# A newly searched order of steps for a fused linear-attention and gated-convolution kernel

## The chip, the cores and the metric

The kernel runs on one core of a Trainium2 chip. The metric is the device time of one execution in microseconds. Five engines work side by side, each through its own instructions in order: TensorE (PE, matmuls and the loading of their weights), VectorE (DVE), ScalarE (ACT), GpSimd (POOL) and SyncE (SP), which here only issues transfers. Transfers are carried out by 16 DMA engines. The profile is one execution recorded by the hardware profiler.

## The reference

For each of 8 batches there is an attention over 8 heads, 576 positions and head dimension 64, in which the scores are replaced by features; its result goes through a gated long convolution.

```python
def phi(x):
    proj = np.einsum('bhsd,df->bhsf', x, w_phi)                  # 64 -> 128
    proj = proj - np.max(np.abs(proj), axis=-1, keepdims=True)
    return np.concatenate([np.exp(proj), np.exp(-proj)], axis=-1)
q_p, k_p = phi(q), phi(k)
kv  = np.einsum('bhsf,bhsd->bhfd', k_p, v)
z   = np.sum(k_p, axis=2)
num = np.einsum('bhsf,bhfd->bhsd', q_p, kv)
den = np.einsum('bhsf,bhf->bhs', q_p, z)[..., None] + 1e-06
x   = (num / den) -> (8, 576, 512)

proj = x @ w_proj                                                # 512 -> 3 * 512
x1, x2, x3 = the three thirds of proj
x2_conv = irfft(rfft(x2, axis=1) * rfft(filter_fft, axis=0), n=576, axis=1)
out = (x1 * x2_conv * x3) @ w_out                                # (8, 576, 512)
```

Inputs and output are float32; the kernel computes its matmuls in bfloat16.

## The kernel before

The kernel is a list of words, `PLAN`, written out in full at the top of the file. Each word is the name of a small method with its arguments, and after an `@` the PSUM bank that it writes or reads. `run()` goes through the list once and calls them, so the list is the order in which every engine gets its instructions. Within one engine nothing overtakes; between engines an instruction waits only for what it reads or overwrites.

```python
for word in PLAN.split():
    name, _, bank = word.partition("@")
    self.bank = int(bank) if bank else None
    f, *args = name.split(",")
    getattr(self, f)(*[int(a) if a.isdigit() else a for a in args])
```

The first number of a word is the batch. Words that name an engine (`ACT`, `DVE`, `POOL`, `SP`) run there; the others have a fixed engine. The steps of one batch b, with the lines that the profile gives for them:

- `load` (L555), `loadh` (L561), `w_load` (L545, L548): q, k, v and the weights come from HBM, converted to bfloat16, by transfers that GpSimd issues. q, k, v have two buffers each.
- `trh` (L567): half of q or k is transposed by a DMA that SyncE issues; for batch 0 TensorE does it (`pt`, L577) and an engine copies the result out (`pte`, L296 on ScalarE, L298 on VectorE, which are the copies of all steps).
- `Pk`, `Qn` (L596, L603), `Pkt`, `Qnt` (L611): feature projections in the natural layout; `maxk`, `maxq`, `maxkt`, `maxqt` (VectorE, L672) take the maxima of the absolute values, `ex`, `exkt`, `exqt` (ScalarE, L658, L661, L666) the exponentials. `mhi`, `mlo`, `trm`, `trme` bring the maxima of q into rows. `Pq`, `Pqt` (L630, L636, L643, L647) project q again, transposed, with the maxima subtracted.
- `em` (L708) and `vs` (L714): v is scaled by the exponential of the maximum.
- `KV` (L729), `KVe` (copy), `NE`, `NEt` (L743, L752): the two contractions of the attention; `rc`, `xn`, `rct`, `xnt` (VectorE, L757 to L774) divide. The result x of the batch lies in four tiles `xn` and a smaller `xnt`.
- `trx` (L781), `trxt` (L786): x is transposed into `xT`, `xTt` by DMAs that SyncE issues. `ptx` (L791), `ptxt` (L800) do the same on TensorE, with `ptxe`, `ptxte` as copies out of PSUM.
- `f1`, `f2` (L811, L817): sums and differences of x; `F` (L823, L827), or `Ft` and `Fs` (L836, L843) for two tiles together: the transform along the positions; `Fe`, `Xl` copy it.
- `X2` (L862) projects in the frequency domain, `Y1` (L867, L872) multiplies by the filter's transform, `m3` (L876) adds.
- `X1`, `X3` (L884), `X1t`, `X3t` (L893) project x for the gates, with `X1e`, `X1te` (copies) and `tm`, `tmt` (L925, L929), which multiply. Each X1 and each X3 reads all four transposed tiles of the batch.
- `I` (L937), or `It` and `Is` (L944, L951): inverse transform, then `Ie` (L955, ScalarE), `Ip`, `Im` (L958, VectorE) and `ym` (L1003). `J` (L993) does the inverse with ten matmuls instead of six and needs only `yj` (L997) after it.
- `O` (L1014), `Oe` (copy), `st` (L1023): output projection, copy, and two half stores, issued by SyncE, the last five by ScalarE.

`wz` (L315) multiplies zeros by zeros, twice per word; its number is only a label. Before the first batch the kernel also builds the cosine and sine matrices of the transforms and transforms the filter (`ang`, `frac`, `sin`, `Hd`, `He`, `fa`, `hg`).

The batches overlap: while one batch's convolution runs, the attention of the next one or two is under way.

Of the kernel before, what the change touches and what calls it, by code (L numbers as in the profile page):

```python
# [49 lines left out]
fa,POOL,1 ptx,0,2@7 rc,0,0@0 ex,k,p,1,0@4 NEt,0@2 xn,0,0@0 rct,0@2 ptxe,ACT,0,2@7 ptx,0,0@6  # L50
xnt,0,1@2 ptx,0,3@4 xnt,0,0@2 Pk,1,3@0 ptxe,ACT,0,3@4 ptxe,DVE,0,0@6 fa,POOL,0 Pkt,1@2 Qn,1,2@6
X1,0,3@4 maxq,1,2@6 sin,4 X1,0,0@5 maxk,1,3@0 load,k,2 Hd,1@6 w_load,proj,1 Hd,0@7 X1e,DVE,0,3@4
exkt,m,1@2 He,DVE,1,1@6 f1,POOL,0,0,0 X3,0,0@4 X1e,ACT,0,0@5 He,DVE,1,0@6 exkt,p,1@2 Hd,2@5
ex,k,p,1,3@0 f1,POOL,0,0,1 f1,DVE,0,1,0 Hd,3@6 He,ACT,2,0@5 f1,POOL,0,1,1 ex,k,m,1,3@0 maxkt,1@2
tm,0,0@4 Pk,1,2@2 hg,ACT X1,0,2@0 f2,POOL,0,0,0 maxk,1,2@2 Qn,1,1@4 f2,POOL,0,0,1 He,DVE,3,0@6
Hd,4@1 ex,k,m,1,2@2 f2,DVE,0,1,1 em,m,1,0 em,p,1,0 ex,k,p,1,2@2 f2,DVE,0,1,0 vs,POOL,p,1,0
X1e,DVE,0,2@0 trh,k,2,0 He,ACT,3,1@6 maxq,1,1@4 X3,0,3@0 He,ACT,0,0@7 trh,k,2,1 em,p,1,1
He,ACT,4,0@1 F,0,3@4 vs,POOL,m,1,0 tm,0,3@0 F,0,1@6 Fe,ACT,0,3@4 ptxt,0@1 F,0,0@2 trh,q,2,0
Fe,ACT,0,1@6 F,0,2@4 ptxte,ACT,0@1 Fe,DVE,0,0@2 em,m,1,1 mhi,1 load,v,2 Fe,ACT,0,2@4 Pk,2,0@6
Pk,2,1@2 trh,q,2,1 KV,1,0@0 maxk,2,0@6 Xl,ACT,0 gen_ends,POOL maxk,2,1@2 X2,0,1@4 ex,k,p,2,0@6  # L60
mlo,POOL,1 load,k,3 X2,0,0@5 ex,k,m,2,0@6 KVe,DVE,1,0@0 vs,POOL,m,1,1 late Y1,0,1@4 Pkt,2@0 trm,1@6
X2,0,3@7 trme,ACT,1@6 exkt,m,2@0 Y1,0,0@5 X2,0,4@4 ex,k,p,2,1@2 w_load,out X2,0,2@6 maxkt,2@0
ex,k,m,2,1@2 vs,POOL,p,1,1 Y1,0,4@4 X1t,0@5 exkt,p,2@0 Y1,0,2@6 Pq,1,0@2 em,m,2,0 Pq,1,1@0
ex,q,m,1,0@2 X1te,DVE,0@5 X3,0,2@4 m3,POOL,0,0 Y1,0,3@7 ex,q,p,1,0@2 X1,0,1@5 tm,0,2@4 ex,q,p,1,1@0
Pq,1,2@2 m3,DVE,0,1 load,k,4 Qn,2,1@6 ex,q,m,1,1@0 X3,0,1@4 maxq,2,1@6 vs,POOL,m,2,0 X1e,ACT,0,1@5
NE,1,0@0 ex,q,m,1,2@2 tm,0,1@4 X3t,0@5 I,0,0@6 rc,1,0@0 tmt,0@5 xn,1,0@0 Ie,0,0@6 I,0,1@4 Im,0,0@6
trx,1,0 Ie,0,1@4 I,0,2@0 Ip,0,0@6 ex,q,p,1,2@2 Im,0,1@4 ym,POOL,0,0 NE,1,1@6 Ip,0,1@4 Ie,0,2@0
Pq,1,3@4 em,p,2,0 rc,1,1@6 xn,1,1@6 KV,1,1@2 load,q,3 ex,q,m,1,3@4 Im,0,2@0 trx,1,1 vs,POOL,p,2,0
Ip,0,2@0 Pk,2,2@6 ex,q,p,1,3@4 J,0,3@0 maxk,2,2@6 KVe,ACT,1,1@2 NE,1,3@2 ex,k,p,2,2@6 ym,POOL,0,2
yj,0,3@0 NE,1,2@4 rc,1,3@2 ex,k,m,2,2@6 KV,2,0@0 rc,1,2@4 xn,1,3@2 ym,POOL,0,1 xn,1,2@4 trx,1,3  # L70
Qn,2,0@6 Pqt,1@2 KVe,ACT,2,0@0 f1,POOL,1,1,1 maxq,2,0@6 O,0,3@4 exqt,m,1@2 trx,1,2 exqt,p,1@2
Pk,2,3@0 f1,POOL,1,0,0 Qnt,2@6 Qn,2,3@2 ex,k,p,2,3@0 maxqt,2@6 O,0,0@5 f1,POOL,1,0,1 maxq,2,3@2
Oe,ACT,0,3@4 trh,q,3,0 O,0,2@6 f1,DVE,1,1,0 O,0,1@4 Oe,ACT,0,2@6 f2,DVE,1,0,0 f2,POOL,1,1,1
trh,q,3,1 maxk,2,3@0 Oe,ACT,0,0@5 NEt,1@2 Oe,ACT,0,1@4 Qn,2,2@5 f2,POOL,1,1,0 rct,1@2 X1,1,3@7
trh,k,3,1 ex,k,m,2,3@0 xnt,1,0@2 xnt,1,1@2 X1,1,2@4 maxq,2,2@5 f2,POOL,1,0,1 X1e,ACT,1,3@7
st,SP,0,3,0 F,1,2@0 X1e,DVE,1,2@4 trh,k,3,0 mhi,2 F,1,3@6 Fe,ACT,1,2@0 mlo,DVE,2 F,1,0@2
Fe,DVE,1,3@6 em,p,2,1 trm,2@0 F,1,1@4 vs,POOL,p,2,1 trxt,1 trme,ACT,2@0 Fe,DVE,1,0@2 Pq,2,1@6
Fe,ACT,1,1@4 Qn,3,2@0 Qn,3,0@2 ex,q,p,2,1@6 st,SP,0,1,0 maxq,3,2@0 X2,1,2@4 st,SP,0,3,1 load,v,3
ex,q,m,2,1@6 X2,1,0@5 maxq,3,0@2 load,q,4 em,m,2,1 Pq,2,0@6 vs,POOL,m,2,1 Y1,1,0@5 Pq,2,2@0
ex,q,p,2,0@6 X2,1,3@2 Y1,1,2@4 ex,q,m,2,0@6 X2,1,1@5 ex,q,p,2,2@0 Y1,1,3@2 NE,2,0@6 X1,1,1@4  # L80
ex,q,m,2,2@0 Y1,1,1@5 m3,POOL,1,1 X3,1,2@2 Xl,ACT,1 X1e,ACT,1,1@4 NE,2,1@0 tm,1,2@2 Pkt,3@4
X3,1,3@3 rc,2,0@6 exkt,p,3@4 rc,2,1@0 xn,2,0@6 exkt,m,3@4 X1,1,0@2 xn,2,1@0 trx,2,0 tm,1,3@3
f1,POOL,2,0,0 Pqt,2@0 maxkt,3@4 KV,2,1@6 trx,2,1 exqt,p,2@0 m3,POOL,1,0 exqt,m,2@0 Pq,2,3@4
X1e,ACT,1,0@2 trh,k,4,1 Pk,3,1@0 ex,q,m,2,3@4 X2,1,4@2 maxk,3,1@0 f1,POOL,2,0,1 KVe,ACT,2,1@6
X3,1,0@3 st,SP,0,2,0 Y1,1,4@2 ex,q,p,2,3@4 NE,2,2@6 f2,POOL,2,0,1 tm,1,0@3 ex,k,m,3,1@0 X3,1,1@2
rc,2,2@6 xn,2,2@6 I,1,1@4 f2,POOL,2,0,0 tm,1,1@2 trx,2,2 Ie,1,1@4 NE,2,3@6 ex,k,p,3,1@0 Ip,1,1@4
X1t,1@2 rc,2,3@6 Im,1,1@4 X3t,1@3 X1te,ACT,1@2 xn,2,3@6 NEt,2@4 tmt,1@3 I,1,0@0 trx,2,3 rct,2@4
ym,POOL,1,1 xnt,2,1@4 Ie,1,0@0 I,1,3@6 xnt,2,0@4 Ip,1,0@0 Ie,1,3@6 trxt,2 Pk,3,2@4 Im,1,0@0
Pk,3,0@2 Im,1,3@6 ex,k,m,3,2@4 ym,POOL,1,0 J,1,2@0 Ip,1,3@6 maxk,3,0@2 st,SP,0,0,1 ex,k,p,3,2@4
st,SP,0,1,1 ym,POOL,1,3 X1,2,0@6 yj,1,2@0 trh,k,4,0 ex,k,p,3,0@2 X3,2,0@7 maxk,3,2@4 X1e,ACT,2,0@6  # L90
F,2,0@0 st,SP,0,2,1 yt,ACT,1 O,1,0@6 ex,k,m,3,0@2 f1,DVE,2,1,0 st,SP,0,0,0 Fe,DVE,2,0@0 trh,q,4,1
em,m,3,0 Pk,3,3@4 f1,DVE,2,1,1 Qn,3,3@2 ex,k,m,3,3@4 f2,DVE,2,1,0 O,1,1@0 f2,POOL,2,1,1 maxq,3,3@2
trh,q,4,0 em,p,3,0 X1,2,2@1 Oe,ACT,1,0@6 vs,POOL,p,3,0 maxk,3,3@4 O,1,2@6 X1e,ACT,2,2@1 st,SP,1,0,0
tm,2,0@7 F,2,1@2 st,SP,1,0,1 ex,k,p,3,3@4 X1,2,1@1 Oe,DVE,1,2@6 vs,POOL,m,3,0 Fe,ACT,2,1@2
Oe,DVE,1,1@0 Ft,2,1,6@4 X1e,ACT,2,1@1 Qn,3,1@2 Fs,2,2@4 maxq,3,1@2 Fs,2,3@6 O,1,4@1 Fe,ACT,2,2@4
load,v,4 Fe,ACT,2,3@6 Qnt,3@2 em,m,3,1 Qn,4,0@4 Xl,DVE,2 Pkt,4@6 maxqt,3@2 X2,2,3@0 exkt,m,4@6
maxq,4,0@4 mhi,3 exkt,p,4@6 X3,2,2@2 mlo,POOL,3 vs,POOL,m,3,1 em,p,3,1 Oe,DVE,1,4@1 X2,2,2@3
Y1,2,3@0 st,SP,1,4,1 trm,3@1 KV,3,0@4 trme,ACT,3@1 load,q,5 maxkt,4@6 Pq,3,0@0 Y1,2,2@3 load,k,5
KVe,ACT,3,0@4 Pq,3,1@6 Pq,3,2@4 load,k,6 ex,q,p,3,1@6 tm,2,2@2 X2,2,1@3 vs,DVE,p,3,1 ex,q,m,3,1@6
X3,2,1@2 ex,q,m,3,0@0 X2,2,0@6 tm,2,1@2 ex,q,p,3,0@0 O,1,3@7 Y1,2,1@3 ex,q,p,3,2@4 NE,3,1@0  # L100
Y1,2,0@6 X1,2,3@3 ex,q,m,3,2@4 X3,2,3@2 rc,3,1@0 m3,POOL,2,0 X1e,ACT,2,3@3 xn,3,1@0 Oe,ACT,1,3@7
Qn,4,2@4 trx,3,1 Pq,3,3@0 maxq,4,2@4 KV,3,1@6 ex,q,m,3,3@0 m3,POOL,2,1 st,SP,1,3,1 tm,2,3@2 Qnt,4@4
ex,q,p,3,3@0 X2,2,4@3 maxqt,4@4 KVe,ACT,3,1@6 NE,3,0@0 Y1,2,4@3 Pk,4,1@6 rc,3,0@0 NE,3,2@4
# [973 lines left out]
```

## Time and profile before

| | |
|---|---|
| runs | 302.89, 303.11, 308.19 us; median 303.11 |
| profiled execution | 304.44 us, of which the span from the first to the last instruction is 302.7 |
| busy us in the span | PE 275.4, DVE 260.4, ACT 225.8, POOL 208.8 |
| mean granted TensorE clock | 0.982 of full |
| bytes moved | 40.12 MB, mean 133 GB/s |
| words in the order | 1,483 |

In a window view each engine has its busy time and, in brackets, its number of instructions. A matmul's recorded time is longer than the time until the next one can start, so a busy TensorE is not yet a TensorE at its limit; the length of a step is read from the chain of waits, where a piece lasts until the next one begins. A row of a wait names who waited, for whom, how long in total, how often and at most.

### The profile page before, as it was taken

How to read it: one execution, taken by the hardware profiler on the slowest of the kernel's cores; microseconds unless marked ns; L12 is line 12 of the kernel's file. 1: busy time of each engine (PE TensorE's matmuls, PEld its weight loads, DVE VectorE, ACT ScalarE, POOL GpSimd, SP SyncE). 2: the span in 40 equal slices, each digit the busy share in tenths (PEclk: the TensorE clock that was granted, in tenths of full speed). 3: DMA queues.
4: the chain of work that ended last, by engine and by line, in shares of the span. 5: the costliest groups of instructions: out<-in, count | busy, mean ns of one | idle time of the engine just before them, and what ended most of it. 6: DMA issues, size and time to landing. Idle time of an engine off the chain costs nothing.

```text
span 302.7 us, 10174 instructions
## 1 busy us (share of the span) xinstructions
PE 275.4 (91%) x4287; PEld 201.3 (67%) x4316; DVE 260.4 (86%) x440; ACT 225.8 (75%) x361; POOL 208.8 (69%) x168
## 2 busy tenths in 40 slices
...
GB/s 135 191 191 185 186 205 170 159 160 119 107 159 202 117 114 155 175 176 119 200 167 151 106 111 106 155 194 118 132 76 69 71 89 64 20 98 2 90 63 196
DMA packets 72446, 40.12 MB, mean 133 GB/s; under 512 B 52752, under 2 KB 67216, under 8 KB 72400
## 3 DMA queue, kind: packets, MB, share of 16 engines
...
q8 instruction: 33, 0.54, 0.8%
q10 hardware_dynamic: 400, 0.66, 0.8%
...
HBM read 33.75 MB, written 9.44 MB: 143 GB/s over the span
## 4 chain that ended last, share of the span: by engine, by line
PE 72%; ACT 9%; DVE 8%; DMA 5%; issue 3%; POOL 2%; SPq 0%; DVEq 0%; ACTq 0%
PE ps L884 17%; PE ps L862 12%; PE ps L1014 9%; PE ps L729 5%; PE ps L937 5%; PE ps L743 4%; DMA xT<-xn 3%; PE ps L603 2%; PE ps L630 2%; DVE mq L672 2%; PE ps L893 2%; PE ps L827 2%; PE ps L596 2%; PE ps L823 2%; PE ps L636 2%
## 5 line engine op out<-in xcount | busy, mean ns | idle before, releaser
L884 PE MATMUL ps<-xT,wproj 128*128 128x256 bf16 x512 | 64.2, 273 | 3.4 <-DMA xT<-xn 3.3
L884 PEld LDWEIGHTS <-wproj 128*128 128x128 bf16 x512 | 48.3, 98 | 13.6 <-issue 4.1
L672 DVE TENSOR_REDUCE mq<-ps 128x8 f32<-128x1024 f32 (+1 forms) x40 | 43.7, 1112 | 5.2 <-PE ps L603 2.5
L672 DVE TENSOR_REDUCE mk<-ps 128x8 f32<-128x1024 f32 (+1 forms) x40 | 44.2, 1112 | 4.6 <-PE ps L596 3.3
L1003 POOL TENSOR_TENSOR yT<-cv,x1s 128x576 bf16<-128x576 f32 x24 | 30.8, 1298 | 18.2 <-DVE x1s L929 9.5
L817 POOL TENSOR_TENSOR xf<-SD 128x512 bf16<-128x512 bf16 x25 | 29.1, 1177 | 14.3 <-DVE SD L811 13.7
L876 POOL TENSOR_TENSOR T<-T,T 128x1024 bf16<-128x1024 bf16 x14 | 29.6, 2122 | 13.2 <-DVE T L872 13.2
L714 POOL TENSOR_TENSOR vp<-vn,vp 128x1152 bf16<-128x1152 bf16 x14 | 30.2, 2154 | 9.0 <-ACT vp L708 9.0
L658 ACT ACTIVATE Eqp<-ps 128x1024 bf16<-128x1024 f32 x32 | 32.6, 1040 | 4.8 <-PE ps L636 4.8
L658 ACT ACTIVATE Eqm<-ps 128x1024 bf16<-128x1024 f32 x32 | 32.7, 1041 | 4.6 <-PE ps L636 4.6
L714 POOL TENSOR_TENSOR vm<-vn,vm 128x1152 bf16<-128x1152 bf16 x16 | 35.1, 2197 | 1.0 <-ACT vm L708 0.7
L658 ACT ACTIVATE Ekp<-ps 128x1024 bf16<-128x1024 f32 x32 | 33.0, 1035 | 2.9 <-PE ps L596 1.9
L1014 PE MATMUL ps<-wout,yT 128*128 128x512 bf16 x132 | 34.1, 380 | 0.9 <-POOL xf L817 0.2
L658 ACT ACTIVATE Ekm<-ps 128x1024 bf16<-128x1024 f32 x32 | 33.1, 1036 | 1.4 <-DVE mk L672 0.9
L862 PE MATMUL ps<-wproj,XF 128*128 128x512 bf16 x119 | 30.0, 380 | 0.6 <-issue 0.2
L811 POOL TENSOR_TENSOR SD<-xn 128x512 bf16<-128x512 bf16 x20 | 23.0, 1171 | 9.2 <-DVE xn L762 7.8
L296 ACT CAST x1s<-ps 128x512 bf16<-128x512 f32 (+1 forms) x32 | 17.9, 560 | 14.9 <-PE ps L884 7.9
L958 DVE TENSOR_TENSOR cv<-es,ps 128x288 f32<-128x288 f32 x52 | 21.2, 445 | 4.0 <-PE ps L862 1.4
L925 DVE TENSOR_TENSOR x1s<-ps,x1s 128x512 bf16<-128x512 f32 x32 | 21.8, 683 | 3.0 <-PE ps L884 2.1
L762 DVE TENSOR_TENSOR xn<-ps,r 128x512 bf16<-128x512 f32 x32 | 21.8, 688 | 1.0
L743 PE MATMUL ps<-KVs,Eqp 128*128 128x65 bf16 x256 | 20.5, 195 | 1.7 <-ACT Eqp L658 0.9
L1014 PEld LDWEIGHTS <-yT 128*128 128x128 bf16 x144 | 12.9, 98 | 13.5 <-POOL yT L1003 0.8
(177 smaller groups left out, 673.5 us busy)
## 6 DMA issues: line engine op xcount, KB each, us to landing
...
```

The source lines that it names most:

```text
L658: self.nc.scalar.activation(e, p, AF.Exp, bias=0.0, scale=1.0 if g == "p" else -1.0)
L672: self.nc.vector.tensor_reduce(out=out, in_=src, axis=AX.X, op=ALU.max, apply_absolute_value=True)
L714: self.eng(eng).tensor_tensor(out=t[:, :, :, 0:64], in0=self.at("vn", b)[:, 2 * X:2 * X + 2], in1=t[:, :, :, 64:65].to_broadcast([128, 2, ...
L743: self.mm(self.pb(u, 65 * a, 65 * a + 65), E, KVs[:, u, v, s, :], start=(s == 0), stop=(s == 1))
L762: self.nc.vector.tensor_tensor(out=o, in0=n[:, :, :, 0:64], in1=self.at("r", 4 * b + v).to_broadcast([128, 2, 4, 64]), op=ALU.mult)
L811: self.eng(eng).tensor_tensor(out=o[:, :, 2 * i:2 * i + 2, :], in0=x[:, :, 0:2, :], in1=x[:, :, 2:4, :], op=ALU.subtract if i else ALU.add)
L817: self.eng(eng).tensor_tensor(out=o[:, :, 2 * i:2 * i + 2, :], in0=x[:, :, 0:4:2, :], in1=x[:, :, 1:4:2, :], op=ALU.subtract if i else ALU ...
L862: self.mm(self.pb(0), l, w[:, kt, 512:1024], start=(kt == 0), stop=(kt == 3))
L876: self.eng(eng).tensor_tensor(out=Y, in0=Y, in1=self.at(f"T{2 * e + 1}", b), op=ALU.add)
L884: self.mm(o[:, d], w[:, kt, f0 + 128 * m:f0 + 128 * m + 128], y[:, 1, ::-1, ::-1] if d else y[:, 0], start=(kt == 0), stop=(kt == 3))
L1003: self.eng(eng).tensor_tensor(out=self.at("yT", b)[:, m, 0:SEQ], in0=self.turn_of("cv", (b, m)).rearrange("p x h t -> p (x h t)"), in1=sel ...
L1014: self.mm(self.pb(0), y[:, kt, 128 * c:128 * c + 128], w[:, kt, :], start=(kt == 0), stop=(kt == 3))
```

## The change

Only the list `PLAN` is replaced, by one found in a new search. The search counts two things anew: that VectorE's instructions, of every form, may have to wait while GpSimd issues a transfer, and that transposes by DMA are halted while an engine's instructions are fetched. All methods stay. The new list has 1,486 words.

Almost every word moves. Beside the places, these numbers change (before, after):

| words | before | after |
|---|---|---|
| `trx` / `ptx` | 29 / 3 | 27 / 5 |
| `trxt` / `ptxt` | 7 / 1, batch 0 by `ptxt` | 7 / 1, batch 2 by `ptxt` |
| `F` / `Ft` / `Fs` | 30 / 1 / 2 | 32 / 0 / 0 |
| `I` / `It` / `Is` / `J` | 24 / 2 / 2 / 6 | 23 / 4 / 4 / 5 |
| `wz` | 9 | 6 |
| `X1e` on ACT / DVE | 27 / 5 | 21 / 11 |
| `KVe` on ACT / DVE | 9 / 7 | 12 / 4 |
| `Fe` on ACT / DVE | 21 / 11 | 23 / 9 |
| `vs` on POOL / DVE | 30 / 2 | 28 / 4 |
| `m3` on POOL / DVE | 14 / 2 | 12 / 4 |
| `f1` on POOL / DVE | 20 / 12 | 25 / 7 |
| `f2` on POOL / DVE | 25 / 7 | 22 / 10 |

The places that the prediction speaks of, from the diff of the list:

```diff
-ident wz,18@0 frac,3 load,q,1 wz,2@1 load,v,0 frac,1 ang,DVE,2 pt,q,0,0,0@0 sin,3 w_phi zeros
...
-maxqt,0@2 Pkt,0@0 ex,k,p,0,2@6 trh,q,1,0 maxkt,0@0 wz,20@2 maxk,0,1@4 ex,k,m,0,2@6 Pk,0,3@2
-trh,q,1,1 maxk,0,3@2 ex,k,p,0,1@4 em,p,0,0 em,m,0,0 gen_neg,DVE wz,22@4 mhi,0 exkt,p,0@0 maxk,0,2@6
-mlo,POOL,0 vs,POOL,m,0,0 ex,k,p,0,3@2 trh,k,1,0 trm,0@5 wz,3@4 vs,DVE,p,0,0 trme,ACT,0@5
...
-exqt,m,0@6 xn,0,2@0 NE,0,3@2 exqt,p,0@6 load,q,2 NE,0,0@0 rc,0,3@2 ex,k,m,1,0@4 xn,0,3@2 wz,29@6
...
-X1t,2@1 trx,3,3 Im,2,3@2 J,2,0@6 Ip,2,3@2 X1te,ACT,2@1 tmt,2@0 st,SP,1,2,1 Im,2,2@4 ym,POOL,2,3
-I,2,1@0 Ip,2,2@4 st,SP,1,2,0 yj,2,0@6 Ie,2,1@0 Pk,4,0@4 st,SP,1,1,0 Qn,4,3@2 ym,POOL,2,2 Im,2,1@0
-ex,k,p,4,0@4 X1,3,2@6 st,SP,1,4,0 Ip,2,1@0 maxq,4,3@2 trh,k,5,0 ex,k,m,4,0@4 X1,3,1@7 ym,POOL,2,1
...
-X3,3,3@0 ex,k,m,5,1@2 Im,3,1@4 f1,POOL,4,1,0 Ip,3,1@4 trx,4,3 Pqt,4@6 tm,3,3@0 I,3,0@4 exqt,m,4@6
-ym,POOL,3,1 maxk,5,1@2 exqt,p,4@6 J,3,2@0 st,SP,2,1,1 Ie,3,0@4 st,SP,2,3,1 Im,3,0@4 load,q,7
-Ip,3,0@4 Pk,5,3@2 yj,3,2@0 It,3,3@6 Pkt,5@4 Is,3,3@6 exkt,p,5@4 X3,4,3@0 Ie,3,3@6 maxkt,5@4
...
+pte,DVE,k,0,1,1@4 Qn,0,2@2 maxqt,0@0 Pk,0,1@4 ex,k,m,0,0@6 maxq,0,2@2 Qn,0,3@0 trh,q,1,0
+ex,k,m,0,1@4 Pkt,0@6 maxq,0,3@0 Pk,0,2@2 ex,k,m,0,2@2 trh,k,1,1 maxkt,0@6 wz,12@0 ex,k,p,0,2@2
+maxk,0,1@4 Pk,0,3@0 exkt,p,0@6 trh,q,1,1 ex,k,p,0,1@4 maxk,0,3@0 mhi,0 em,m,0,0 maxk,0,2@2
+mlo,POOL,0 ex,k,m,0,3@0 trh,k,1,0 vs,POOL,m,0,0 trm,0@4 wz,19@5 trme,ACT,0@4 ang,DVE,4 em,p,0,0
...
+xn,2,3@0 Ie,1,3@4 X3t,1@2 NEt,2@6 Im,1,3@4 trx,2,3 f1,POOL,2,1,1 Ip,1,3@4 I,1,1@0 rct,2@6 tmt,1@2
+Ie,1,1@0 J,1,0@4 xnt,2,1@6 ym,POOL,1,3 trh,k,4,0 xnt,2,0@6 Im,1,1@0 Ip,1,1@0 Pk,3,2@6 yj,1,0@4
+Pk,3,0@2 ym,POOL,1,1 st,SP,0,1,0 ex,k,p,3,2@6 I,1,2@0 trh,q,4,1 maxk,3,0@2 X1,2,0@4 Ie,1,2@0
...
+tm,2,0@5 load,k,5 F,2,1@2 Fe,ACT,2,3@0 F,2,2@6 load,q,5 Fe,DVE,2,1@2 O,1,4@5 Fe,ACT,2,2@6
...
+em,p,3,1 vs,POOL,p,3,1 Pq,3,1@6 trh,k,5,1 tm,2,2@4 KVe,ACT,3,0@2 Pq,3,2@0 Y1,2,2@5 ex,q,p,3,1@6
...
+Ie,2,3@2 maxk,4,1@4 f1,POOL,3,1,0 X1te,ACT,2@0 I,2,2@6 Ie,2,2@6 trh,k,5,0 ptx,3,3@0 f1,POOL,3,0,0
+tmt,2@1 J,2,0@4 ptxe,ACT,3,3@0 Ip,2,3@2 Im,2,3@2 Im,2,2@6 st,SP,1,3,0 ym,POOL,2,3 I,2,1@2 Ip,2,2@6
+st,SP,1,3,1 yj,2,0@4 Ie,2,1@2 Pk,4,0@6 st,SP,1,4,1 Qn,4,3@0 ym,POOL,2,2 Ip,2,1@2 ex,k,m,4,0@6
+X1,3,2@4 Im,2,1@2 maxq,4,3@0 ex,k,p,4,0@6 X1,3,1@5 ym,POOL,2,1 X1e,ACT,3,2@4 Pqt,3@0 maxk,4,0@6
...
+Pqt,4@6 xn,4,3@0 Ie,3,1@2 exqt,p,4@6 maxk,5,1@4 It,3,2@0 trx,4,3 f1,POOL,4,1,1 exqt,m,4@6 Is,3,2@0
+Ie,3,2@0 X3,3,3@6 Im,3,1@2 st,SP,2,0,0 Ip,3,1@2 Im,3,2@0 I,3,0@4 ym,POOL,3,1 st,SP,2,3,1 tm,3,3@6
+Ie,3,0@4 ptx,4,2@2 trh,k,6,0 Ip,3,2@0 Pk,5,3@6 ptxe,DVE,4,2@2 Pkt,5@0 ym,POOL,3,2 Im,3,0@4 I,3,3@2
+exkt,m,5@0 Ip,3,0@4 st,SP,2,0,1 exkt,p,5@0 X1,4,3@4 ym,POOL,3,0 Ie,3,3@2 ex,k,m,5,3@6 Ip,3,3@2
```

299 lines of the change are left out of this document (147 added, 152 removed).

## The prediction

> **What bounds the kernel now.** I read the page's engine rows first, then ten-microsecond windows, then the chain of waits around the two places where the windows sag. The page's first row and its shares of the chain:
>
> ```profile
> PE 275.4 (91%) x4287; PEld 201.3 (67%) x4316; DVE 260.4 (86%) x440; ACT 225.8 (75%) x361; POOL 208.8 (69%) x168
> PE 72%; ACT 9%; DVE 8%; DMA 5%; issue 3%; POOL 2%; SPq 0%; DVEq 0%; ACTq 0%
> ```
>
> TensorE (PE) carries 72% of the chain that sets the end, VectorE (DVE) 8%, transfers 5%. The windows (columns: span of the window, busy us and instructions of PE, weight loads, DVE, ACT, POOL, granted clock, DMA share, GB/s) say where TensorE is not full:
>
> ```profile
> 20.00:30.00 10.00, 7.53 (x177) 5.65 (x177) 9.21 (x11) 9.84 (x18) 8.19 (x6) 0.73 1.05 176
> 30.00:40.00 10.00, 7.34 (x169) 6.32 (x164) 6.99 (x13) 7.61 (x11) 6.67 (x6) 0.83 1.26 191
> 160.00:170.00 10.00, 9.95 (x249) 8.06 (x243) 9.64 (x18) 7.99 (x11) 7.90 (x7) 1.00 0.95 132
> 170.00:180.00 10.00, 7.60 (x81) 6.14 (x82) 7.62 (x15) 5.56 (x11) 4.35 (x4) 1.00 0.85 121
> ```
>
> The window from 160 us is what the steady part looks like: TensorE 9.95 of 10. Two things stand out against it: the first 40 us, where ScalarE and VectorE feed TensorE through start-up (5.1 us idle in the two windows shown), and the hole at 170 us. The waits of PE and the timeline name the hole and a smaller one at 141 us:
>
> ```profile
> PE ps L884 <- DMA xT<-xn: 3.3, 2, 2.4
> 141.95 1.58 PE L884 MATMUL ps<-xT,wproj 128*128 128x256 bf16 x13 [0.90 <-DMA xT<-xn]
> 176.34 2.45 PE L884 MATMUL ps<-xT,wproj 128*128 128x256 bf16 x21 [2.40 <-DMA xT<-xn]
> ```
>
> Both are the projection matmuls (L884) waiting for the last DMA transpose of xn into xT (L781). They cost 3.3 us together and are the only transfers for which TensorE stands still for more than half a microsecond after start-up.
>
> **Why those two were late.** The order gives every transpose a lead: the TensorE work that stands between its word and the first word that reads xT. Service times of the steps, from the chain in order of time (start, us, what; in the L596 row half the records are absent):
>
> ```profile
> 290.75 1.23 PE ps L993 x10
> 168.45 0.73 PE ps L937 x6
> 143.86 0.22 PE ps L596 x8
> 169.18 0.87 PE ps L884 x8
> 138.35 3.55 DMA xT<-xn
> 170.48 5.82 DMA xT<-xn
> ```
>
> Between trx,3,3 and X1,3,2 the old order has J,2,0, I,2,1, Pk,4,0 and Qn,4,3 (a Qn has as many matmuls of the same size as a Pk): 1.23 + 0.73 + 0.22 + 0.22 = 2.40 us. The transfer needed 3.55, so 1.15 short; 0.90 was waited. For trx,4,3 the lead is 3.15, the transfer took 5.82, 2.67 short, 2.40 waited. The lead reckoning gives the stalls to within 0.3 us, so I use it for the new order.
>
> **The change part by part.** Only the order and the assignment of some steps to engines change. *TensorE's work* stays: two F and two PE transposes (ptx) more, one Ft and two Fs fewer, one I and one J fewer, two It/Is pairs more; by the step lengths of the chain that is within 0.1 us of nothing. Six filler matmuls go (nine wz words become six). They lay in start-up waits:
>
> ```profile
> L315 PE MATMUL ps<-zz 128*128 128x512 bf16 x15 | 6.5, 539 | 7.7 <-DVE zz L310 6.1 <-ACT Ekp L658 1.2 <-DVE mq L672 0.3
> L791 PE MATMUL ps<-ident,xn 128*128 128x128 bf16 x12 | 1.2, 250 | 0.2 <-issue 0.2
> ```
>
> so I take 0; at most 6 x 0.54 = 3.2 us would be gained, and if they held the clock up something is lost (a rival below).
>
> *Transposes.* trx,3,3 and trx,4,2 become PE transposes with an evacuation; the place of the 0.90 stall is thus gone. Its stand-in, ptx,3,3, keeps the same 2.40 us of TensorE work behind it and needs about 0.25 + 0.59 us. trx,4,3 stays a DMA with a lead of 3.38 instead of 3.15. By the same count the new order leaves four leads under 4 us: 3.13 (trx,2,3: I, J, two Pk, I), 3.38 (trx,4,3), 3.59 (trx,1,3), 3.81 (trx,3,2). What a landing takes is in the two source views:
>
> ```profile
> DMA to landing us min/median/max: 2.4/3.3/9.5
> DMA to landing us min/median/max: 3.2/3.8/6.1
> ```
>
> (first L781, then L567, the transposes of k and q). With half of the landings past 3.3 us, I let half of the four be late, at the mean of the two rows above (4.7): (1.6 + 1.3 + 1.1 + 0.9) / 2 = 2.4 us lost. Bounds: 0 if all land at the minimum of 2.4, and 9.4 if each takes 5.82. So the transposes give -3.3 + 2.4 = -0.9. In start-up trh,q,1,0 has 2.33 us of lead where it had 3.74; against the median of 3.8 that is 1.4 us more short, but TensorE idles there a quarter of the time anyway: +0.3, bounds 0 and +1.4. Further on, trh,k,5,1 now stands 6.5 us of TensorE work behind its load (load,k,5), so SyncE may wait there some 2 us, with trx,3,1 queued behind; that one has 8.85 us of lead, so this costs 0, and up to 2 if that cover were gone.
>
> *Engine shares.* Rows of the groups, same step on either engine:
>
> ```profile
> L714 POOL TENSOR_TENSOR vp<-vn,vp 128x1152 bf16<-128x1152 bf16 x14 | 30.2, 2154 | 9.0 <-ACT vp L708 9.0
> L714 DVE TENSOR_TENSOR vp<-vn,vp 128x1152 bf16<-128x1152 bf16 x2 | 4.0, 1994 | 0.0
> L876 POOL TENSOR_TENSOR T<-T,T 128x1024 bf16<-128x1024 bf16 x14 | 29.6, 2122 | 13.2 <-DVE T L872 13.2
> L876 DVE TENSOR_TENSOR T<-T,T 128x1024 bf16<-128x1024 bf16 x2 | 2.3, 1163 | 0.0
> L811 POOL TENSOR_TENSOR SD<-xn 128x512 bf16<-128x512 bf16 x20 | 23.0, 1171 | 9.2 <-DVE xn L762 7.8 <-DVE r L757 1.4
> L811 DVE TENSOR_TENSOR SD<-xn 128x512 bf16<-128x512 bf16 x12 | 6.3, 541 | 0.2
> L817 DVE TENSOR_TENSOR xf<-SD 128x512 bf16<-128x512 bf16 x7 | 3.2, 475 | 0.1
> L298 DVE CAST x1s<-ps 128x512 bf16<-128x512 f32 x5 | 3.4, 681 | 0.7 <-PE ps L884 0.7
> L298 DVE CAST KVs<-ps 128x520 bf16<-128x520 f32 x7 | 4.8, 692 | 0.0
> L298 DVE CAST XF<-ps 128x576 bf16<-128x576 f32 x11 | 8.1, 753 | 2.4 <-PE ps L827 1.5 <-ACT XF L296 1.0
> ```
>
> VectorE: six X1e (+4.1), two vs (+4.0), two m3 (+2.3), three f2 (+1.4) come; five f1 (-2.7), three KVe (-2.1), two Fe (-1.5) go: +5.5 us. GpSimd loses two vs (-4.3), two m3 (-4.2), three f2 (-3.5) and gains five f1 (+5.9) and a ym: about -5. ScalarE changes by about -1. With the chain's shares, 8% of 5.5 is +0.4 and 2% of 5 is -0.1. Bounds: 0 and +5.5 (all on the path, as where a stage is VectorE's).
>
> *VectorE's waits behind GpSimd.* The new search counts them. What the old order suffers:
>
> ```profile
> 21.89 2.14 POOL L714 TENSOR_TENSOR vm<-vn,vm 128x1152 bf16<-128x1152 bf16 x1
> 23.98 0.81 POOL L545 DMA_DIRECT2D wproj<-in_moe_w_proj_dram  x1
> 22.61 2.64 DVE L714 TENSOR_TENSOR vp<-vn,vp 128x1152 bf16<-128x1152 bf16 x1
> ```
>
> The DVE multiplication is held from 22.61, and with vs on DVE averaging 1.99 over two, the other one took 1.35; 23.9 + 1.35 = 25.25 is when it ended, so it was GpSimd's vm, over at 24.03, that held it and not the issue that follows until 24.79. What the search can save behind issues is therefore small: I take -0.2, bounds 0 and -1.3 (one such hold, 2.64 less 1.35). [...]
>
> **The sum.** -0.9 + 0.3 + 0.4 - 0.1 - 0.2 = -0.5 us against the profiled execution, 304.4 us (span 302.7 and 1.7 around it), so 303.9. The median of the runs is 303.1, 1.3 lower; the same difference gives **302.6 us**, no change that can be told. A measurement of this kernel tells about 2%, 6.1 us: 297.0 and 309.2 are the borders.
>
> **Rivals.**
> *A, the short leads are caught (slower).* All four transposes of leads 3.13 to 3.81 take what the one at 170 us took, 5.82: 2.69 + 2.44 + 2.23 + 2.01 = 9.4 instead of 2.4, so 302.6 + 7.0 = 309.6. It decides from three late by two microseconds on. For it: the longest landing is 9.5. Against: the median is 3.3. Chance 0.15.
> *B, the clock.* Three windows of before:
>
> ```profile
> 18.70:22.10 3.40, 1.81 (x11) 0.66 (x11) 3.40 (x5) 3.23 (x8) 0.43 (x2) 0.50 1.26 156
> 22.10:25.50 3.40, 3.40 (x45) 2.30 (x45) 3.15 (x2) 3.40 (x7) 3.26 (x3) 0.52 1.12 218
> 35.80:39.20 3.40, 3.18 (x43) 2.85 (x42) 1.70 (x4) 2.96 (x5) 3.40 (x2) 0.53 1.30 194
> ```
>
> The granted clock is half for about 10 us, after stretches where TensorE was half idle, and the old order puts filler at 21 to 23 and at 37 us; the new one has none after about 22 us. If one to two more such stretches of 6.8 us run at half rate, steps that fill 7.4 of 10 us there take up to twice as long: 6.8 x (2 x 0.74 - 1) = 3.3 us each, so 302.6 + 3.3 = 305.9, with two 309.2. Against: ScalarE and VectorE, not TensorE, are the full engines there. Chance 0.12, a third of it past the border. [...]
> *C, VectorE becomes the bound.* All 5.5 us fall on the path: 302.6 + 5.1 = 307.7. For it: 9.64 of 10 at 160 us. Against: 8% of the chain. Chance 0.08.
> *D, the search is right (faster).* No new stall (-3.3), half of the 5.1 us of start-up idle and the 0.8 us that remains of the window from 190 us as waits go too: 303.1 - 3.3 - 2.6 - 0.8 = 296.4. For it: every one of these is idle time of TensorE. Against: start-up is full on ScalarE. Chance 0.18.
>
> ```profile
> 190.00:200.00 10.00, 9.17 (x245) 6.56 (x245) 8.15 (x12) 8.14 (x11) 8.10 (x5) 1.00 1.13 173
> ```
>
> *E, the order does not do what it says:* stalls elsewhere of the same size, 303.1. Chance 0.07.
>
> **How the numbers follow.** The forecast has the rest, 0.40, with its own range of 299 to 306. Past 309.2 lie A, a third of B, a quarter of C and a little of the forecast's tail: 0.15 + 0.04 + 0.02 + 0.03 = 0.24. Below 297.0 lie D and a hundredth more: 0.19. The rest, 0.57, is within 2%. The range that leaves 2 in 10 out, from a part of D to A: 296.5 to 309.5.
>
> **What would show it.** Right: PE's waits name xT<-xn with 2 to 3 us, in the places of trx,4,3 or trx,2,3, and none at X1,3,2; DVE busy near 266, POOL near 204; PE's share of the chain still above 70%. Wrong: xT waits of 0 or above 6 us; a clock under 0.8 in windows past 40 us; DVE's share of the chain doubled; TensorE's idle time in 10 to 40 us changed by more than 2 us.

## The result and the profile after

The new order is slower: 317.23 us, median of 4 runs (316.42 to 319.07), against 303.00 for the order before beside it; ratio 1.0481 [1.0424, 1.0538]. The profiled execution took 317.37 us with a span of 315.6, 12.9 more than before. Some executions of each of these kernels take some 1.5 to 4% longer than its fastest; medians are over all runs, ratios, with their 95% intervals, leave those out.

The page after, the row of the engines and the shares of the chain:

```profile
PE 280.6 (89%) x4314; PEld 203.2 (64%) x4314; DVE 271.8 (86%) x449; ACT 224.8 (71%) x358; POOL 203.5 (64%) x167
PE 80%; DVE 12%; issue 5%; ACT 1%; DMA 1%; DVEq 0%
```

Transfers fell from 5% of the chain to 1%, VectorE rose from 8% to 12% and "issue" from 3% to 5%. Issue is time in which an engine waits for nothing that the profile shows. Of the waits of PE:

```profile
PE ps L637 <- issue: 3.5, 2, 2.6
PE ps L730 <- DVE vp L715: 3.1, 1, 3.1
PE ps L730 <- issue: 2.7, 1, 2.7
PE ps L938 <- issue: 1.0, 1, 1.0
```

The wait for xT that was 3.3 us before is in no row. Beside small ones of the start-up (2.2 us for mh at most), two kinds have come instead: one wait for VectorE's vp, and several for "issue". (Lines are one higher than before: KV is L730, Pq L631 and L637.)

**The start-up.** KV,0,0 begins at 29.2 us (25.4 before), NEt,0 at 44.9 (38.5). VectorE and GpSimd in the timeline:

```profile
23.35 4.53 DVE L423 TENSOR_SCALAR turn<-fr,cols 128x288 f32<-128x288 f32 x2
27.80 1.35 DVE L715 TENSOR_TENSOR vp<-vn,vp 128x1152 bf16<-128x1152 bf16 x1
...
22.63 2.15 POOL L715 TENSOR_TENSOR vm<-vn,vm 128x1152 bf16<-128x1152 bf16 x1
24.72 0.81 POOL L546 DMA_DIRECT2D wproj<-in_moe_w_proj_dram  x1
25.54 2.17 POOL L715 TENSOR_TENSOR vm<-vn,vm 128x1152 bf16<-128x1152 bf16 x1
```

The pair of L423 is the word ang,DVE,4. Of the two instructions the first ran from 23.35 to 24.95, as GpSimd's first vm ended, and the second from 24.87 to 27.88, as the second vm ended; the same form at 7.16 us took 0.82 for two. vp and KV,0,0 come behind it. The windows show what follows:

```profile
20.00:30.00 10.00, 4.74 (x74) 3.10 (x75) 10.00 (x8) 8.69 (x16) 7.55 (x6) 0.51 1.06 181
30.00:40.00 10.00, 6.45 (x182) 5.69 (x177) 8.18 (x9) 5.46 (x6) 8.85 (x7) 0.67 1.20 223
40.00:50.00 10.00, 8.99 (x127) 7.30 (x126) 9.27 (x17) 8.41 (x11) 4.48 (x4) 0.80 1.22 184
```

TensorE is busy 4.74 us where it was 7.53, and its clock is 0.51, 0.67 and 0.80 where it was 0.73, 0.83 and 1.00.

**The halts.** The chain in order of time, at the two largest:

```profile
80.41 0.58 PE ps L730 x30
81.00 2.71 issue
83.70 0.85 PE ps L730 x42
...
205.43 0.11 PE ps L631 x2
205.53 2.63 issue
208.16 0.39 PE ps L637 x3
```

TensorE stops in the middle of KV,2,0, behind the 30th of 72 equal matmuls, and in the middle of Pq,5,2. No operand is missing. What arrives shortly before it goes on is a packet of instructions. The queue of TensorE's instructions on the page (packets, MB, share of the DMA engines), and behind it all queues in two windows, 202.4 to 205.5 us and 205.5 to 206.8:

```profile
q8 instruction: 33, 0.54, 0.7%
```

```profile
q1 hardware_dynamic: 855, 0.66, 89.8%
q0 software_dynamic: 119, 0.12, 24.1%
...
q1 hardware_dynamic: 625, 0.17, 192.0%
q8 instruction: 1, 0.02, 5.5%
```

33 packets of 16 KB stand beside 8,628 recorded TensorE instructions, 261 each, so I estimate a packet at 256 instructions of 64 bytes. Counting TensorE's records in order of start bears it out: six halts come behind instructions whose number leaves 192 when divided by 256 (1984, 2752, 4032, 5056, 5824, 6848). I count the packet needed there as due when TensorE crosses the boundary before. From the packets and the instructions (us):

| due | packet begins | ends | TensorE halts | goes on | converting load in flight |
|---|---|---|---|---|---|
| 76.8 | 79.8 | 82.2 | 80.8 | 83.7 | load,k,4 |
| 103.4 | 106.5 | 107.4 | 107.9 | 108.8 | load,v,4 |
| 141.7 | 147.9 | 148.9 | 148.9 | 150.2 | load,v,5 |
| 175.0 | 177.4 | 178.6 | 179.2 | 180.0 | load,v,6 |
| 202.3 | 205.6 | 206.7 | 205.3 | 208.2 | load,k,7 |
| 240.3 | 243.0 | 243.9 | 244.3 | 245.4 | load,v,7 |

From 103.6 to 106.4 us and from 240.4 to 243.0 us no packet of q1 was under way, and q0 took 118.0% and 91.4% of the engines' time: there a load alone delayed the fetch. At 202.3 the last packets of load,k,7 ended at 204.3, and transposes and stores went on until the fetch began.

Each time TensorE goes on 1.3 to 1.5 us behind the end of the packet. From one matmul to the next the halts are 2.89, 0.88, 1.28, 0.81, 2.89 and 1.09 us, together 9.8. The order before has two such halts, which its waits of PE show:

```profile
PE ps L636 <- issue: 1.5, 1, 1.5
PE ps L743 <- issue: 0.8, 1, 0.8
```

They are at 31.2 and 196.1 us, 1.77 and 0.97 from one matmul to the next, 2.7 together. So two theories: **H**, VectorE is held behind GpSimd in the start-up; **F**, converting loads in flight (q0) delay the fetches of TensorE's instructions, and a fast stretch then runs out of them. Rivals to F are **D**, the fast stretches outrun any fetch, and **T**, the transposes (q1) delay it. **S** is used later: a load in flight slows a transpose.

### The profile page after: what moved, and what is told of

It reads as the page before. It is cut to its first block, busy times and chain, and to the rows that moved or that the text cites. A ratio compares the mean times of both kernels' runs of the same rounds, so it can differ in the third digit from the quotient of the medians.

```text
span 315.6 us, 10204 instructions
## 1 busy us (share of the span) xinstructions
PE 280.6 (89%) x4314; PEld 203.2 (64%) x4314; DVE 271.8 (86%) x449; ACT 224.8 (71%) x358; POOL 203.5 (64%) x167
## 4 chain that ended last, share of the span: by engine, by line
PE 80%; DVE 12%; issue 5%; ACT 1%; DMA 1%; DVEq 0%
PE ps L885 18%; PE ps L863 11%; PE ps L1015 10%; PE ps L730 6%; PE ps L938 5%; PE ps L744 5%; PE ps L824 3%; PE ps L828 3%; PE ps L631 2%; PE ps L597 2%; PE ps L894 2%; PE ps L637 2%; PE ps L604 2%; PE ps L994 2%; DVE mk L673 2%
## 5 line engine op out<-in xcount | busy, mean ns | idle before, releaser
L812 POOL TENSOR_TENSOR SD<-xn 128x512 bf16<-128x512 bf16 x25 | 28.5, 1152 | 27.5 <-DVE xn L763 21.9
L1004 POOL TENSOR_TENSOR yT<-cv,x1s 128x576 bf16<-128x576 f32 x25 | 31.7, 1276 | 11.6 <-DVE x1s L926 6.1
L715 POOL TENSOR_TENSOR vm<-vn,vm 128x1152 bf16<-128x1152 bf16 x15 | 32.3, 2150 | 8.9 <-ACT vm L709 8.9
L715 POOL TENSOR_TENSOR vp<-vn,vp 128x1152 bf16<-128x1152 bf16 x13 | 28.5, 2195 | 13.6 <-ACT vp L709 13.4
L1015 PE MATMUL ps<-wout,yT 128*128 128x512 bf16 x144 | 36.9, 389 | 0.0
L877 POOL TENSOR_TENSOR T<-T,T 128x1024 bf16<-128x1024 bf16 x12 | 25.9, 2166 | 9.3 <-DVE T L873 9.0
L818 POOL TENSOR_TENSOR xf<-SD 128x512 bf16<-128x512 bf16 x22 | 25.5, 1174 | 7.6 <-DVE SD L812 3.7
L297 ACT COPY o<-ps 128x512 f32<-128x512 f32 x25 | 14.6, 592 | 17.5 <-PE ps L1015 16.9
L959 DVE TENSOR_TENSOR cv<-es,ps 128x288 f32<-128x288 f32 x54 | 21.9, 447 | 3.4 <-ACT es L956 3.2
L1015 PEld LDWEIGHTS <-yT 128*128 128x128 bf16 x144 | 12.9, 99 | 13.6 <-issue 1.5
L744 PE MATMUL ps<-KVs,Eqp 128*128 128x65 bf16 x256 | 21.3, 201 | 0.3 <-DVE KVs L299 0.2
```

Of the source, the lines that this page charges most:

```text
L715: self.eng(eng).tensor_tensor(out=t[:, :, :, 0:64], in0=self.at("vn", b)[:, 2 * X:2 * X + 2], in1=t[:, :, :, 64:65].to_broadcast([128, 2, ...
L744: self.mm(self.pb(u, 65 * a, 65 * a + 65), E, KVs[:, u, v, s, :], start=(s == 0), stop=(s == 1))
L812: self.eng(eng).tensor_tensor(out=o[:, :, 2 * i:2 * i + 2, :], in0=x[:, :, 0:2, :], in1=x[:, :, 2:4, :], op=ALU.subtract if i else ALU.add)
L818: self.eng(eng).tensor_tensor(out=o[:, :, 2 * i:2 * i + 2, :], in0=x[:, :, 0:4:2, :], in1=x[:, :, 1:4:2, :], op=ALU.subtract if i else ALU ...
L877: self.eng(eng).tensor_tensor(out=Y, in0=Y, in1=self.at(f"T{2 * e + 1}", b), op=ALU.add)
L1004: self.eng(eng).tensor_tensor(out=self.at("yT", b)[:, m, 0:SEQ], in0=self.turn_of("cv", (b, m)).rearrange("p x h t -> p (x h t)"), in1=sel ...
```

## The experiments

### One word earlier in the start-up

```diff
-vs,POOL,m,0,0 trm,0@4 wz,19@5 trme,ACT,0@4 ang,DVE,4 em,p,0,0
+vs,POOL,m,0,0 trm,0@4 wz,19@5 trme,ACT,0@4 em,p,0,0
-sin,0 frac,3 pt,k,0,0,0@2
+sin,0 frac,3 ang,DVE,4 pt,k,0,0,0@2
```

> The new order with one word moved: ang,DVE,4, the VectorE instruction pair that took 4.53 us at 23.35 us behind GpSimd's vm, issue of w_proj and vm, stands right behind frac,3, where the same form took 0.82 us. Theory H (VectorE's SBUF-to-SBUF work is held while GpSimd works back to back): the pair takes under 1 us, vp of the first batch starts near 24 us instead of 27.8 or is itself held by about 1.3 as in the old order, KV,0,0 begins 2 to 4 us earlier, and 2 to 4 of that reach the end: 313 to 315 us, unless the six halts of TensorE eat or add some. Rival (that stretch was bound by the clock or by exponentials): under 1 us of 317.2 changes.

312.11 us; ratio to the order before 1.0272 [1.0201, 1.0343], clear of the new order's interval. The timeline:

```profile
23.69 2.25 DVE L715 TENSOR_TENSOR vp<-vn,vp 128x1152 bf16<-128x1152 bf16 x1 [0.29 <-ACT vp L709]
```

vp is itself held by 0.9, yet KV,0,0 begins at 26.0 instead of 29.2, and NEt,0 at 37.9 instead of 44.9: with TensorE busy for 6.76, 8.62 and 9.73 us of the three windows from 20 to 50 us (4.74, 6.45 and 8.99 in the new order) the clock is 0.72, 0.83, 1.00. The gain, 5.1 us by the medians and 2.1% by the ratios, is more than the 2 to 4 us expected, which had left out the clock that follows the hold. H holds. The halts stay, 11.3 us together in this profile.

### One load later

```diff
-trme,ACT,5@2 load,k,7 Pq,5,0@4
+trme,ACT,5@2 Pq,5,0@4
-m3,POOL,4,1 st,SP,3,1,1
+m3,POOL,4,1 load,k,7 st,SP,3,1,1
```

> The new order with one word moved: load,k,7, issued at 197.1 us with packets until about 204, goes behind m3,POOL,4,1, so is issued near 204.5. Theory F (TensorE runs out of fetched instructions, because a fetch that starts while GpSimd's converting loads send packets begins 2.4 to 3.7 us late, against 0.3 to 1.0 without them): the fetch that began at 205.61 begins near 203.3, the halt of 2.89 us in Pq,5,2 shrinks to under 1 us, and the whole is 2 to 2.9 us shorter: 314.3 to 315.3. Rival D (the dense stretch of 256 instructions in 2.94 us outruns any fetch) or rival T (the transposes of qT in flight delay it): the halt stays above 2 us and the time within 0.7 us of 317.2. Everything up to 195 us is alike.

The halt in Pq,5,2 fell from 2.89 to 0.67 us (206.54 to 207.21), the packet beginning at 204.36. The median is 318.49; the ratio, 1.0408 [1.0314, 1.0501], is in the direction expected but not apart from the new order's. SyncE's transfers filled the engines here too (q1 took 104.3% from 202.8 to 204.4 us, q0 nothing), so the load made most of this halt. It may have acted in part through the transposes: the first of the two of q landed after 3.2 us, where it had taken 7.6 beside the load.

### Thirteen loads moved

```diff
-load,k,4 (behind m3,POOL,0,1)     +load,k,4 load,v,3 (behind f2,POOL,1,1,0)
-load,v,3 load,q,4 load,v,4        +load,q,4 (m3,POOL,1,1)  load,k,5 load,v,4 (f2,POOL,2,0,0)
-load,k,5 load,q,5                 +load,q,5 (f2,POOL,2,1,1)
-load,k,6 load,v,5                 +load,k,6 (ym,POOL,2,2)  load,v,5 (f2,POOL,3,1,0)
-load,q,7 load,v,6 load,q,6        +load,v,6 (f1,POOL,4,1,1) load,q,6 (ym,POOL,3,3) load,q,7 (f2,POOL,4,1,1)
-load,k,7 load,v,7                 +load,k,7 (m3,POOL,4,1)  load,v,7 (ym,POOL,4,0)
```

> The new order with 13 loads of q, k and v moved to places where TensorE works through 256 instructions slowly, so that none sends packets while a fetch for a dense stretch is due (76.8, 103.4, 141.7, 175.0, 202.3, 240.3 us). Theory F: the six halts at every 256th instruction, 2.89, 0.88, 1.28, 0.81, 2.89 and 1.09 us, together 9.8, shrink to under 2.5 together, and 6 to 8 us of it reach the end: 309 to 311.5 us. Rival D: the halts stay, 316 to 318. Rival T (transposes delay the fetches): about half stays, since the transposes stay where they are: 313 to 315. A load that now comes too late for its transpose or its scaling would show as a new wait of TensorE on qT, kT or vp.

The waits of PE:

```profile
PE ps L885 <- DMA xT<-xn: 5.6, 1, 5.6
PE ps L730 <- DVE vp L715: 3.1, 1, 3.1
PE ps L637 <- issue: 0.4, 1, 0.4
```

Five of the six halts are gone and the sixth is 0.65 us, with every transpose word in its place: D and T fall as the main cause. The 0.65 that is left, and the halt of 0.97 in the order before, stand with no load under way: the packets began 0.7 and 1.2 us late, and 256 instructions were worked off in 2.9 and 2.7 us. There D is enough. But the time is 316.79, ratio 1.0437 [1.0360, 1.0514]: the gain was turned into a new wait of 5.6 us for xT. The expectation had named waits for a load that comes too late (qT, kT, vp); this one is a transpose of x, beside which loads now run, as the next run shows.

### Both edits

```diff
+the edits of a1_turn_early and a3_loads
```

> Both edits together, ang,DVE,4 early and the 13 loads moved. Theories H and F together: the gains add, 8 to 12 us: 305 to 309 us, within 2 of the order before (303.0). What is then left over it is the slower clock between 20 and 50 us and single waits. If the two gains overlap (the start-up's delay only moves the place of the halts), 309 to 312.

310.48 us, ratio 1.0225 [1.0187, 1.0262], 1.5 us past the range, with the same wait for xT, 5.7 us here. The issues to landings from 100 to 113 us (transfers, KB, median us):

```profile
kn<-in_k_dram POOLq DMA_DIRECT2D x1, 576.0 KB, 6.4
vn<-in_v_dram POOLq DMA_DIRECT2D x1, 576.0 KB, 10.1
xT<-xn SPq DMA_TRANSPOSE x2, 6.3
kT<-kn SPq DMA_TRANSPOSE x1, 9.4
```

load,k,5 and load,v,4 now ran beside the transposes of batch 2; one xT took 9.9 us, where the median was 3.3 before.

### The same loads elsewhere, twice

```diff
-f2,POOL,2,0,0 load,k,5 load,v,4 ... f2,POOL,2,1,1 load,q,5
+f2,POOL,2,1,1 load,k,5 load,q,5 ... vs,POOL,m,3,0 load,v,4
```

> The kernel with both edits (310.48 us), in which the loads of k and v of batches 5 and 4 were issued at 101.7 and 102.5 us, while xT of batch 2 was being transposed: one transpose took 9.9 us to land and TensorE waited 5.7 us for it at 107. Here load,k,5 and load,q,5 stand behind f2,POOL,2,1,1 and load,v,4 behind vs,POOL,m,3,0. Theory S (a transpose is slowed by a load beside it, so the gain of the halts was turned into that wait): the wait goes to under 1 us, 304 to 306 us. Rival: the wait only moves, to kT or qT of the next batch, 308 to 310.5.

The wait moved, as the rival had it: in the profile TensorE waits 5.8 us for a kT that landed after 12.4 us. The median is 310.69. The ratio, 1.0038 [0.9987, 1.0090], is of the four runs from 304.0 to 307.1 us; the profile is of one of the other six, 310.4 to 312.8, and that only those have the wait is not shown. Then load,k,5 and load,q,5 went back to their places of the new order, behind vs,POOL,m,3,0, and load,v,4 behind mlo,POOL,3:

```diff
-f2,POOL,2,1,1 load,k,5 load,q,5 ... vs,POOL,m,3,0 load,v,4 ... mlo,POOL,3
+f2,POOL,2,1,1 ... vs,POOL,m,3,0 ... load,k,5 ... load,q,5 ... mlo,POOL,3 load,v,4
```

> The new order with ang,DVE,4 early and 11 loads moved; load,k,5 and load,q,5 are back at their places of the new order (behind vs,POOL,m,3,0, after the transposes of k of batch 4) and load,v,4 stands behind mlo,POOL,3. In b1_loads_again the runs fell into two groups, 304.0 to 307.1 and 310.4 to 312.8 us, and a profiled one of the slower group had a wait of 6.0 us of TensorE at 117 us for a kT whose transpose took 12.4 us beside load,k,5 and load,q,5. Theory S: that wait is gone in every run, 303 to 306 us, no second group from it, the halts at every 256th instruction under 2 us together; so all of the 14 us between the orders is found. Rival: another transpose takes it over, 308 or more.

303.53 us, ratio 1.0023 [0.9979, 1.0067]. The waits of PE:

```profile
PE ps L730 <- issue: 1.4, 1, 1.4
PE ps L612 <- DMA kT<-kn: 1.0, 1, 1.0
```

The places of one VectorE word and eleven loads account for the difference between the two orders. One halt of 1.56 us at 132.8 beside load,v,4 stood out; that word was moved on:

```diff
-mlo,POOL,3 load,v,4 ... ym,POOL,2,3
+mlo,POOL,3 ... ym,POOL,2,3 load,v,4
```

> c1_loads_third with load,v,4 moved from behind mlo,POOL,3 (issued 122.2 us, packets until 134) to behind ym,POOL,2,3, about 142.8, where TensorE takes some 8 us for 256 instructions. Theory F: the halt of 1.56 us at 132.8 is gone and no other takes its place, 1 to 1.5 us shorter than c1_loads_third: ratio to the order before 0.996 to 1.000. Rival: vs of batch 4, which needs v at 152, waits, no gain or up to 2 us slower.

303.69 us, ratio 0.9983 [0.9946, 1.0020]: the ratio expected, the halt gone, a wait of 1.3 for yT in another place, and no gain over the 303.53 that the runs can show. The other words of the new order, mended in this way, are worth nothing that can be measured.

### Fillers

```diff
+wz,22@5 (behind em,m,0,0)  +wz,3@5 (behind wz,19@5)  +wz,29@5 (behind Qn,1,3@6)
```

> The same as b1_loads_again with three more fillers wz, where the order before had them: ahead of mhi,0, behind the transposed maxima, and near 37 us. Theory C (the lower granted clock from 20 to 40 us, 0.66 against 0.73 and less in the order with the hold, comes of the missing fillers): the clock from 20 to 30 us rises by 0.1 or more and 0.5 to 1.5 us are gained over b1_loads_again. Rival (the clock followed from the hold, which is mended): within 0.5 us of it, or some tenths slower for the fillers' own 0.4 to 0.9 us each.

311.40 us; the runs of its base, b1_loads_again, lie 8.8 us apart, so it tells nothing. The same three words upon c1_loads_third:

> c1_loads_third with three more fillers wz at the places of the order before. Theory C (missing fillers lower the clock): the granted clock from 20 to 30 us rises by 0.1 or more and 0.5 to 1.5 us are gained. Rival (the clock followed from the hold of VectorE): within 0.5 us of c1_loads_third.

Ratio 1.0013 [0.9965, 1.0061], against 1.0023 without. The windows from 20 and 30 us, first without the fillers, then with:

```profile
20.00:30.00 10.00, 6.96 (x145) 4.90 (x140) 8.74 (x8) 9.57 (x17) 6.10 (x5) 0.66 1.09 174
30.00:40.00 10.00, 7.12 (x198) 6.22 (x194) 9.32 (x18) 9.86 (x13) 8.64 (x8) 1.00 1.37 160
```

```profile
20.00:30.00 10.00, 7.57 (x157) 4.75 (x155) 8.13 (x8) 9.12 (x18) 7.05 (x6) 0.83 1.14 191
30.00:40.00 10.00, 7.33 (x172) 6.20 (x170) 8.31 (x15) 9.00 (x12) 9.32 (x7) 0.83 1.30 202
```

The clock from 20 to 30 us rises by 0.17, as theory C had it, and the one from 30 to 40 us falls by as much; nothing is won. The low clock followed the hold, not the missing fillers: one word moved, in a1_turn_early, brought it from 0.51 to 0.72 without any.

### The other way round: the order before made worse

```diff
-ang,ACT,4 (2nd line)  -frac,4 (behind sin,0)
+wz,3@4 ang,DVE,4 vs,DVE,p,0,0    +frac,4 (behind xn,0,1)
```

> The order before with ang,ACT,4 taken from the first microseconds of ScalarE and put, as ang,DVE,4, ahead of vs,DVE,p,0,0, as the new order has it; frac,4 goes behind xn,0,1. Theory H: the pair is held behind GpSimd's work from 22.6 us to its first gap, 3 to 5 us, vp of the first batch is as much later, and the whole is 2.5 to 5 us slower than the order before: ratio 1.008 to 1.016. Rival (VectorE had slack there): ratio 1.000 to 1.003.

Ratio 0.9998 [0.9951, 1.0045]: a miss for H. The timeline, VectorE and GpSimd:

```profile
23.17 1.86 DVE L422 TENSOR_SCALAR turn<-fr,cols 128x288 f32<-128x288 f32 x2
24.96 1.35 DVE L714 TENSOR_TENSOR vp<-vn,vp 128x1152 bf16<-128x1152 bf16 x1
...
24.54 0.81 POOL L545 DMA_DIRECT2D wproj<-in_moe_w_proj_dram  x1
25.49 2.83 POOL L714 TENSOR_TENSOR vm<-vn,vm 128x1152 bf16<-128x1152 bf16 x1
```

The first of the pair was held to the end of a vm, 1.59 us, exactly as in the new order; the second began 0.14 us into the issue of w_proj, against 0.15 there, and ran in 0.35. Here GpSimd's next vm waited instead (2.83 instead of 2.15). So H is not a matter of the word's place alone: who waits is a close race, and only the new order's profiles lost it. What decides it stays open.

For F, three loads were put on the fetches of fast stretches:

```diff
-load,q,3 (behind KV,1,1@2)   +vs,POOL,m,2,0 load,q,3
-load,v,6 (behind Ip,4,0@2)   +vs,POOL,m,5,0 load,v,6
-load,v,7 (behind KVe,DVE,5,0@1)  +mlo,POOL,6 load,v,7
```

> The order before with three loads moved onto the fetches of dense stretches: load,q,3 from 71.9 to about 68.5 us (fetch due at 71.9), load,v,6 from 211.9 to about 191 (fetch due at 193.3), load,v,7 from 195.2 to about 225.3 (fetches due at 228.1 and 232.0). Nothing else is touched. Theory F: these fetches begin 2.5 to 3 us after they are due instead of 0.5, 1.2, 1.05 and 0.7, TensorE halts 1.5 us at 76, 2.9 instead of 0.97 at 196, 1.4 at 232 and 0.3 at 237, and the whole is 4 to 5.5 us slower: ratio 1.013 to 1.018. Rival (dense stretches or transposes alone decide): ratio 0.997 to 1.003.

Ratio 1.0179 [1.0093, 1.0265], as expected. The waits of PE:

```profile
PE ps L743 <- issue: 3.4, 1, 3.4
PE ps L636 <- issue: 3.2, 2, 2.2
PE ps L729 <- issue: 1.1, 1, 1.1
```

The halts are 1.27, 3.61 and 2.38 us, where 1.5, 2.9 and 1.7 were expected, with packets that began 2.9, 4.1 and 3.8 us late. Loads put on the fetches made the halts in this order, as taking them off unmade those of the new one.

### The order before mended

```diff
-Im,3,0@4 load,q,7 Ip,3,0@4
+Im,3,0@4 Ip,3,0@4 ... f2,POOL,4,1,0 load,q,7
```

> The order before with one load moved: load,q,7, issued at 171.8 us beside two transposes of x of batch 4 that landed after 4.2 and 5.8 us, goes behind f2,POOL,4,1,0, about 184 us. Theory S: the transposes land after 2.4 to 3 us, TensorE's wait for xT at 173.7 (2.4) is gone, and the whole is 1.5 to 2.5 us shorter: ratio 0.992 to 0.995. Rival (the wait is hidden by another, for xn or cv, right behind): ratio 0.998 to 1.001.

```profile
PE ps L743 <- issue: 2.5, 1, 2.5
PE ps L884 <- DMA xT<-xn: 1.3, 2, 0.9
```

The wait of 2.4 at 173.7 is gone, but the load, in flight until 192.3, slowed the transposes of k behind it (6.9 and 5.0 us to land), the packet due at 191.9 began 3.1 us late, and the halt grew from 0.97 to 2.67. From 192.0 to 194.9 us no packet of a load was under way, and q1 took 121.8% of the engines' time: transposes by themselves held a fetch back here, so T is not dead, and F is not the only cause of a halt. Ratio 0.9992 [0.9948, 1.0036], in the rival's range. Then w_load,proj,0 was moved as well:

```diff
-exkt,m,0@0 w_load,proj,0 Pq,0,3@2
+exkt,m,0@0 Pq,0,3@2 ... vs,POOL,p,0,1 w_load,proj,0
```

> d1_old_one_load_off with w_load,proj,0, issued at 24.0 us, moved behind vs,POOL,p,0,1, about 29.3. Theory F: the fetch of TensorE that fell due at 26.2 and began only at 30.46 begins near 27, and the halt of 1.77 us at 31.2 is gone: another 1 to 1.8 us, ratio to the order before 0.987 to 0.992. Rival (w_proj then comes later and the first X1 at 40 us waits for it): no gain over d1 or up to 3 us slower.

Ratio 1.0126 [1.0027, 1.0225]. The halt at 31.2 is gone, as F says (the other one stays, 2.5 us). But the kernel is slower, and not for the rival's reason: VectorE (its first row) met GpSimd at another place.

```profile
32.85 5.07 DVE L298 CAST f<-flt 64x512 bf16<-64x512 f32 x1
...
32.93 4.70 POOL L492 TENSOR_TENSOR fs<-fl 128x1024 bf16<-128x1024 f32 x2
```

The cast, 0.41 us in the order before, was held for the two GpSimd instructions, and TensorE waited 4.7 us for xn. Last, load,q,7 alone, into the gap behind ym,POOL,3,3:

```diff
-Im,3,0@4 load,q,7 Ip,3,0@4 ... ym,POOL,3,3
+Im,3,0@4 Ip,3,0@4 ... ym,POOL,3,3 load,q,7
```

> The order before with load,q,7 moved from 171.8 us to behind ym,POOL,3,3, about 177, after the two transposes of x of batch 4 and with its packets ended by about 186, ahead of the fetch that falls due at 193. Theories S and F together: the wait for xT at 173.7 is gone and the halt at 196 stays at 1.0 (2.67 in d1_old_one_load_off): 1.5 to 2.4 us shorter, ratio 0.992 to 0.995, faster than both kernels. Rival (another wait in that stretch hides it): 0.998 to 1.001.

```profile
PE ps L636 <- issue: 1.5, 1, 1.5
PE ps L884 <- DMA xT<-xn: 0.9, 1, 0.9
PE ps L743 <- issue: 0.9, 1, 0.9
```

The wait at 173.7 is gone and the halt at 194.4 is 1.08; the span is 301.1, 1.6 less. The runs can't show it: ratio 0.9986 [0.9938, 1.0034], outside what was expected and in the rival's range. No version is shown to beat the order before.

### What holds VectorE

```diff
-vs,DVE,p,0,0 ... w_load,proj,0 ... vs,POOL,m,0,1
+vs,DVE,p,0,0 ... vs,POOL,m,0,1 w_load,proj,0
```

> The new order with one word moved: w_load,proj,0, whose issue took GpSimd from 24.72 to 25.53 us between the two vm, goes behind the second vm. Theory I (it is the issue of a transfer that holds VectorE): the pair of ang,DVE,4 takes at most 2 us instead of 4.53 and KV,0,0 begins 2 to 3 us earlier. Theory B (it is held as long as GpSimd's SBUF work follows back to back): the pair still ends only when the second vm does, near 26.9, so takes 3.5 to 3.8, and KV,0,0 begins 0.7 to 1 us earlier, since the issue itself is gone. In both the six halts stay as they are; 314 to 317 us.

Its runs lie from 313.27 to 320.41 us and can't be compared, so only the trace is used:

```profile
22.84 3.97 DVE L423 TENSOR_SCALAR turn<-fr,cols 128x288 f32<-128x288 f32 x2
...
22.32 4.32 POOL L715 TENSOR_TENSOR vm<-vn,vm 128x1152 bf16<-128x1152 bf16 x2
```

With no issue in between, the pair ends at 26.81 us and the two vm at 26.64, as theory B has it: GpSimd's work was enough to hold it. In the new order the second of the pair also stood through the issue between the two vm (24.72 to 25.53 us), in b3_old_turn_late it ran during that issue, in 0.35 us, so an issue lay within the hold in the one and not in the other.

## Why the prediction was wrong

The account by the two profiles: the start-up up to NEt,0 is 6.4 us longer, the halts behind it are 9.8 against 0.97, and the stalls for xT of 3.3 us are gone: 6.4 + 8.8 - 3.3 = 11.9 of the 12.9 us.

- **No term for instruction fetches.** The sum had none. The six halts cost 9.8 us, 7.1 more than the two before, in a span that is 12.9 longer. By the ratios, 1.0481, 1.0272 with the one word moved and 1.0023 with the eleven loads as well, the loads are worth 2.5% and the word 2.1%. The change says that the search counts fetches; I read this as a matter of transposes alone (in the profile after, the median packet of q1 took 0.018 us, and of its 189 packets over 0.9 us 176 overlapped a packet of instructions, q8 or q14) and passed over the "issue" rows in the waits of PE before, which were such halts. In the new order TensorE halted for 0.8 to 2.9 us at six of its 33 packets.
- **"Waits behind GpSimd", -0.2 with bounds 0 and -1.3.** The term had the wrong sign: only what the new order could save was priced. ang,DVE,4 was in the quoted lines of the diff, a step moved from ScalarE to VectorE beside GpSimd's vm, and was not costed. It cost 3.7 us (4.53 less 0.82) and put KV,0,0 back by 3.8.
- **Rival B had the size (3.3 to 6.6 us) and not the cause.** Its clock of about one half came, and with the hold it made NEt,0 6.4 us later; fillers did not mend it, the word in its place did.
- **Transposes: one half right.** The stall of 3.3 us is gone. The four short leads lost 0 instead of 2.4; that holds for these places of the loads, since a3_loads, with the same leads, waited 5.6 us for an xT. Moving the load that slowed the transposes took the larger stall out of the order before too, but its ratio shows no gain.
- **Engine shares.** GpSimd came to 203.5 (204 expected), VectorE to 271.8 (266 expected), 3.7 of the excess being the hold. Rival C did not come: the mended order has 267.5 on VectorE and the old time.
- Of the signs that were to show it wrong, two came: no wait for xT, and TensorE's idle time in 10 to 40 us changed by more than 2 us. The clock past 40 us touched its mark, 0.80 from 40 to 50 us. The remark that half of the L596 records are absent is mistaken: Pk and Qn have eight matmuls each.
